# The first groups of the last expert layer are formed one expert earlier, and the later planner's minor steps go last

## Chip, cores and metric

One core of a Trainium2 chip runs the whole program. The metric is the device time of one execution in microseconds (us). Engines: PE multiplies matrices, DVE (VectorE), ACT (ScalarE) and POOL (GpSimd) work on tiles, SP issues most plain DMAs, POOL the indirect ones.

## What is computed

Three layers follow each other. The kernel's names for the inputs are those of the reference.

```python
x = attention(q, k, v)             # 4 x 8 heads, 576 tokens, 64 wide; block-causal; as (2304, 512)
# first expert layer: two of 8 experts for each token, weights from a softmax over those two
noisy = x @ w_gate + log1p(exp(x @ w_noise)) * noise
x2[token] = sum over its two experts e of  gate * (relu(x[token] @ w1[e]) @ w2[e])
# last expert layer: the best of 8 experts for each token
logits = x2 @ w_gate2 + modality_bias[modality_id]
out[token] = softmax(logits)[best] * (relu(x2[token] @ m2w1[best]) @ m2w2[best])
```

With the reference's inputs the first layer gives its experts 620, 582, 567, 546, 540, 559, 608 and 586 rows. In the last layer only two experts are ever best: number 1 for 1165 tokens and number 2 for 1139. A token is complete once both its first-layer experts have run. After experts 0 to 5, 1188 tokens are complete (588 for expert 1 of the last layer, 600 for expert 2); after experts 0 to 6 there are 1718 (866 and 852).

## The kernel before

**Jobs.** After attention, `run` (L1418) goes through a list of jobs: both parts of experts 0 and 1, then experts 2 to 7 of the first layer (`firsts`, L655), then six jobs of the last layer (`seconds`, L657). A job has up to 620 gathered rows, in tiles of 128 or 124. Its first half (`mm1`, L516, PSUM tile `ph`) makes 8 hidden slices with 24 matmuls each, its second half (`mm2`, L535, PSUM tile `py`, three buffers) 24 matmuls for each row tile. All are split into a high and a low part, so every product is three matmuls. Between the row tiles of one job, `between` (L1440) prepares the next: the columns of its rows (`cols`, L503: 4 transposes into `px`, one ACT copy `xth`, one DVE subtraction `xtl`) and its weight splits (`split`, L454: ACT writes `wh`, and `wl` is a subtraction on POOL for the first layer, on DVE or POOL for the last). `rows` (L1425) gathers the next job's rows on POOL's queue (`gather`, L491, tile `xr`), one for each hidden slice, as soon as the flag that it needs is set. SP fetches weights (`fetch`, L443, tile `raw`), four tiles ahead, when the job's expert is known.

**What a first-layer row tile leaves behind.** POOL adds the finished rows `yr` to X2 in DRAM (`add_rows`, L600). DVE then takes eight dot products of the PSUM tile `py` with the last layer's gate weights (`note`, L570; tile `zero<-py,gts,wide`), and POOL adds them, with a count of one, to LG in DRAM. So column `E` of LG says how many of a token's two experts are done. These dots are fed in between other work (`filler`, L558). Before a new row tile, `room` (L553) issues dots until at most 16 are left, and the PSUM buffer of the tile three back has to be read out first.

**The planner of the last layer.** `gates(k)` (L1478) is a chain of some 60 to 100 small DVE steps with a few matmuls in PSUM tile `pt`, fed in step by step (`walk`, L385). It loads LG on SP's queue (`lgx`), picks each token's best expert, masks the tokens that are complete (L1497), counts, forms full groups of 512 rows of one expert, and turns positions into row lists by one-hot matmuls (`sl_ob`, `sl_ov`, `lists`, `slot_ids`). `eg<k>` says which experts' weights to fetch, `ids<k>0` which rows to gather. k=0 forms two groups of 512 from complete tokens. k=1 forms two more of 512 and two small ones of 256, with an overflow plan (`eo`, `gso`, `more`) that only a loop at the end of the program reads. The chain for k=0 is started when the last dots of expert 6 are placed (`then`, L656), that for k=1 after those of expert 7. PE and DVE take their instructions strictly in the order in which this program writes them, so a matmul of the chain that has to wait holds all of PE.

**Order of transfers.** Gathers of the k=0 groups read X2 while expert 7 may still add rows to it. They touch other tokens, so the program tells the scheduler that these transfers don't depend on each other (L495 to L498, L609): `last_rows` holds expert 7's additions, `early_rows` the gathers.

Of the kernel before, what the change touches and what calls it, by code (L numbers as in the profile page):

```python
# [7 lines left out]
F32 = mybir.dt.float32  # L8
F32R = mybir.dt.float32r
BF16 = mybir.dt.bfloat16  # L10
I32 = mybir.dt.int32
AF = mybir.ActivationFunctionType
OP = mybir.AluOpType
AX = mybir.AxisListType.X
# [16 lines left out]
def moe_kernel(tc, q, k, v, w_gate, w_noise, noise, w1, w2, mod_id, w_gate2, mod_bias, m2w1, m2w2, out):  # L31
    nc = tc.nc
    B, H, S, D = q.shape
    NT, DM = out.shape
    E = w_gate.shape[1]
# [3 lines left out]
    NP = CAP // 128  # L39
# [5 lines left out]
    BW, NW, NSM = GW // 128, 2, 2  # L45
    NV = 5
    NA1 = E * NP
    NTT = NT // 128
# [8 lines left out]
    def bc(ap, shape):  # L57
        return ap.to_broadcast(shape)
# [45 lines left out]
    vec, ten, act = Timed(nc.vector, "dve", dve_cost), Timed(nc.tensor, "pe", pe_cost), Timed(nc.scalar, "act", act_cost)  # L104

    with ExitStack() as top:
# [22 lines left out]
        ones = cst.tile([128, 128], BF16, name="ones")  # L129
# [196 lines left out]
        def starts(pool, n, th, pre):  # L326

            nt = th.shape[1]
            ng = pool.tile([128, E, nt], F32, name=pre + "ng")
            vec.tensor_tensor(ng, bc(n[:, :, None], [128, E, nt]), bc(th[:, None, :], [128, E, nt]), op=OP.is_gt)  # L330
            yield .3
            gn = pool.tile([128, E], F32, name=pre + "gn")
            vec.tensor_reduce(gn, ng, axis=AX, op=OP.add)
            yield .3
            st8 = pool.tile([128, E, E], F32, name=pre + "st8")
            vec.tensor_tensor(st8, lt8, bc(gn[:, None, :], [128, E, E]), op=OP.mult)
            yield .3
            gs = pool.tile([128, E], F32, name=pre + "gs")
            vec.tensor_reduce(gs, st8, axis=AX, op=OP.add)
            yield .3  # L340
            return gn, gs

        def experts_of(pool, gn, gs, dst, pre):

            ge = pool.tile([1, NG2, E], F32, name=pre + "ge")
            vec.tensor_tensor(ge, bc(gs[0:1, None, :], [1, NG2, E]), bc(lane[0:1, 0:NG2, None], [1, NG2, E]), op=OP.is_le)
            yield .3
            ef = pool.tile([1, NG2 + 1], F32, name=pre + "ef")
            vec.tensor_reduce(ef[:, 0:NG2], ge[:, :, 1:], axis=AX, op=OP.add)
            yield .3  # L350
            vec.tensor_tensor(ef[:, NG2:], gs[0:1, E - 1:E], gn[0:1, E - 1:E], op=OP.add)
            yield .3
            vec.tensor_copy(dst, ef)
            yield .3
            return ef[:, NG2:]
# [113 lines left out]
        class Job:  # L469
# [21 lines left out]
            def gather(s, t):  # L491
                xr = rp.tile([128, DM], F32, name="xr", bufs=5)
                i = gps.indirect_dma_start(out=xr, out_offset=None, in_=s.table,
                                                 in_offset=bass.IndirectOffsetOnAxis(ap=s.ic(t), axis=0))
                if s.apart is not None:  # L495
                    for o in s.apart:
                        tc.declare_no_dep(i.ins, o.ins, reason="rows of other tokens")
                    early_rows.append(i)  # L498
                s.xr.append(xr)
                if s is j11:  # L500
                    s.due.append(max(clk["dve"], clk["pool"]) + 2.5)
# [96 lines left out]
        last_rows, early_rows = [], []  # L598

        def add_rows(ids, c0, nt, then=None):  # L600
            last = c0 + nt == NA1
            prev = last_rows if last else []
            placed_ = []

            def f(t, yr, py, g):
                c = c0 + t
                i = gps.indirect_dma_start(out=X2, out_offset=bass.IndirectOffsetOnAxis(ap=ids[:, c:c + 1], axis=0),
                                                 in_=yr, in_offset=None, compute_op=OP.add)
                for o in prev + (early_rows if last else []):  # L609
                    tc.declare_no_dep(i.ins, o.ins, reason="rows of other tokens")  # L610
                prev.append(i)
                note(yr, py, g, ids[:, c:c + 1], placed_, then if t == nt - 1 else None)
            return f

        def job1(e, t0=0, nt=NP, then=None, need=(None, None)):
            return Job((w1[e], w2[e]), X1, nt, lambda t: ids1[:, e * NP + t0 + t:e * NP + t0 + t + 1],
                       lambda t: gts1[:, e * NP + t0 + t:e * NP + t0 + t + 1], add_rows(ids1, e * NP + t0, nt, then), need, 128 if nt == 2 else UNIT)
# [35 lines left out]
        j11.wa, j11.wb = j10.wa, j10.wb  # L653
        chain = lambda k, p: lambda: walk(gates(k), now[0] + .5, p)
        firsts = [job1(0, FIRST[0], NP - FIRST[0], need=(None, "ids1"))]  # L655
        firsts += [job1(e, then={E - 2: chain(0, 1), E - 1: chain(1, 1)}.get(e), need=(None, "ids1")) for e in range(2, E)]  # L656
        seconds = [job2(k, g) for k in range(2) for g in range(NW)] + [job2(1, g, True) for g in range(NSM)]  # L657
        stage = Stage([j00, j10] + firsts + seconds)

# [818 lines left out]
        def gates(k):  # L1478
# [37 lines left out]
            if k == 1:  # L1516
                nr = pool.tile([128, E], F32, name="g_nr")
                vec.scalar_tensor_tensor(nr, gn, -float(GW), pp[:, NTT], op0=OP.mult, op1=OP.add)
                yield .3
                gm, gr = yield from starts(pool, nr, th2, "q_")  # L1520
                yield from experts_of(pool, gm, gr, egs, "q_")
                flags.add("egs")
                vec.tensor_scalar(gr, gr, 2.0, float(BW * NW), op0=OP.mult, op1=OP.add)
                yield .3
                vec.scalar_tensor_tensor(gr, gn, -float(BW), gr, op0=OP.mult, op1=OP.add)
                yield .3
                vec.tensor_add(nr, gs, gn)
                yield .3
                vec.tensor_scalar(nr, nr, NW + .5, 1e5, op0=OP.is_gt, op1=OP.mult)
                yield .3  # L1530
                vec.tensor_add(gs, gs, nr)
                yield .3
                go, s_ = yield from starts(pool, base, th1, "o_")
                vec.tensor_copy(gso, s_)
                yield .3
                yield from experts_of(pool, go, gso, eo, "o_")
            t0, pos, st = tl("t0", sh), tl("pos"), tl("st")
            vec.tensor_tensor(t0, pp[:, 0:NTT], oh, op=OP.mult)
            yield .3
# [14 lines left out]
                vec.scalar_tensor_tensor(w, s2, float(GW), pos, op0=OP.mult, op1=OP.is_gt)  # L1554
                yield .3
            if k == 1:
                vec.tensor_tensor(t0, oh, bc(gr[:, None, :], sh), op=OP.mult)
                yield .3
                vec.tensor_reduce(s2, t0, axis=AX, op=OP.add)
                yield .3  # L1560
                vec.scalar_tensor_tensor(st, st, float(BW), s2, op0=OP.mult, op1=OP.subtract)
                yield .3
                vec.tensor_tensor(st, st, w, op=OP.mult)
                yield .3
                vec.tensor_add(st, st, s2)
                yield .3
# [7 lines left out]
            if k < 2:  # L1574
                new = tl("new") if k else placed
                vec.tensor_scalar(new, a, cap - .5, None, op0=OP.is_lt)
                yield .3
                if k:
                    vec.tensor_add(placed, placed, new)
                    yield .3  # L1580
                    held = tl("held", dt=BF16)
                    vec.tensor_copy(held, placed)
                    yield "pe", 0
                    pm = ps_r.tile([128, NTT], F32, name="pt")
                    ten.matmul(pm, ones, held, start=True, stop=True)
                    yield .4
                    m = pool.tile([1, 1], F32, name="g_m")
                    vec.tensor_reduce(m, pm[0:1], axis=AX, op=OP.add)
                    yield .3
                    vec.tensor_scalar(more, m, float(NT) - .5, None, op0=OP.is_lt)  # L1590
                    yield .3

            vec.tensor_tensor(l, l, bc(mx[:, :, None], sh), op=OP.subtract)
# [11 lines left out]
            for i0_, a0 in enumerate(range(0, cap, 2 * HG)):  # L1605
                na = min(2 * HG, cap - a0)
                pl = ps_r.tile([128, NV, na], F32, name="pt")
                for i in range(2):
                    n = slice(HN * i, HN * i + HN)
                    ob = yield from hot_b(pool, bl[:, n], HN)  # L1610
                    ov = yield from hot_a(pool, a[:, n], HN, a0, na, vals2[:, n])
                    yield from lists(pl, ob, ov, HN, i == 0, i == 1)
                acc = pool.tile([128, NV, na], F32, name="g_acc")
                vec.tensor_copy(acc, pl)
                yield .3
                yield from slot_ids(pool, acc, na, NTT, pad2[:, a0:a0 + na], ids[:, a0:a0 + na], gts[:, a0:a0 + na])
                flags.add("ids%d%d" % (k, i0_ > 0))
            flags.discard("chain")

        with sp():  # L1620
# [131 lines left out]
```

## Time and profile before

| | |
|---|---|
| three runs | 983.49 us median (981.95 to 984.66) |
| the profiled execution | 984.59 us, span 982.8 us |
| PE busy | 943.6 us (96%) |
| DVE, ACT, POOL busy | 681.4 (69%), 482.6 (49%), 489.6 us (50%) |
| share of PE in the chain that ended last | 70% |
| DMA | mean 127 GB/s over the span |

A number such as "668.18" in what follows is a time in us from the start of the span. The rows of a window view give, for each stretch, the busy time of each engine and in brackets its instructions. PEclk is the granted share of PE's full clock (1.00 is 2.4 GHz, 0.50 is 1.2 GHz). A timeline row gives start, duration, engine, line, operation and tiles (out<-in), then in square brackets how long the engine was idle just before, and who ended that. L73 is a helper's line through which every operation goes, so tiles tell them apart.

The stretches of interest: expert 6 takes PE from 610.54 to 668.18, expert 7 to 737.85, the four groups of 512 rows to 785.16, 841.80, 887.25 and 931.74, then come the two small groups.

### The profile page before, as it was taken

How to read it: one execution, taken by the hardware profiler on the slowest of the kernel's cores; microseconds unless marked ns; L12 is line 12 of the kernel's file. 1: busy time of each engine (PE TensorE's matmuls, PEld its weight loads, DVE VectorE, ACT ScalarE, POOL GpSimd, SP SyncE). 2: the span in 40 equal slices, each digit the busy share in tenths (PEclk: the TensorE clock that was granted, in tenths of full speed). 3: DMA queues.
4: the chain of work that ended last, by engine and by line, in shares of the span. 5: the costliest groups of instructions: out<-in, count | busy, mean ns of one | idle time of the engine just before them, and what ended most of it. 6: DMA issues, size and time to landing. Idle time of an engine off the chain costs nothing.

```text
span 982.8 us, 16351 instructions
## 1 busy us (share of the span) xinstructions
PE 943.6 (96%) x5661; PEld 835.6 (85%) x5661; DVE 681.4 (69%) x1676; ACT 482.6 (49%) x1090; POOL 489.6 (50%) x472
## 2 busy tenths in 40 slices
PE   9999998999999999999999999999889988999995
PEld 6989897998978999989898998989767876888894
DVE  6878779888889979395775939577877764433241
ACT  6989997987651344333333333433223332433352
POOL 6234343464325599585875848557374124222122
PEclk9999999999999999999999999999999999999998
DMA  6586742322196366374654627443554525443440
GB/s 128 104 216 192 233 122 70 78 60 68 58 337 156 68 187 165 111 158 97 130 128 116 122 76 171 99 76 47 161 113 124 181 79 175 137 130 108 138 130 13
DMA packets 145293, 124.49 MB, mean 127 GB/s; under 512 B 75626, under 2 KB 115946, under 8 KB 145075
## 3 DMA queue, kind: packets, MB, share of 16 engines
q1 hardware_dynamic: 126242, 90.14, 32.0%
q0 software_dynamic: 17904, 32.96, 16.7%
q8 instruction: 47, 0.77, 0.3%
q10 hardware_dynamic: 1056, 0.26, 0.1%
q14 instruction: 44, 0.35, 0.1%
HBM read 95.50 MB, written 28.09 MB: 126 GB/s over the span
## 4 chain that ended last, share of the span: by engine, by line
PE 70%; issue 11%; DVE 6%; POOL 5%; ACT 4%; DMA 3%; SPq 0%; POOLq 0%; ACTq 0%; DVEq 0%
PE py L73 25%; PE ph L73 25%; PE pt L73 8%; PE ps L73 6%; PE pa L73 3%; POOL wl L73 2%; PE px L73 2%; ACT p L73 2%; DMA raw<-in_moe_w_dram 1%; DVE wl L73 1%; DMA xr<-X,ids 1%; DVE PTl L73 1%; ACT kp L73 1%; DMA qld<-in_q_dram 1%; POOL out_dram L73 1%
## 5 line engine op out<-in xcount | busy, mean ns | idle before, releaser
L73 POOL TENSOR_TENSOR wl<-raw,wh 128x1024 fp32r<-128x1024 f32 x70 | 180.9, 2602 | 113.8 <-ACT wh L73 111.2
L73 DVE SCALAR_TENSOR_TENSOR zero<-py,gts,wide 128x512 f32<-128x512 f32 x304 | 227.6, 749 | 8.4
L73 PE MATMUL ph<-xth,wh 128*128 128x312 f32 (+4 forms) x672 | 217.2, 323 | 2.1 <-DVE kp L73 1.2
L73 PE MATMUL ph<-xtl,wh 128*128 128x312 f32 (+4 forms) x672 | 216.9, 323 | 0.2 <-DVE xtl L73 0.2
L73 PE MATMUL ph<-xth,wl 128*128 128x312 f32 (+4 forms) x672 | 217.1, 323 | 0.0
L73 PE MATMUL py<-wh,kp 128*128 128x512 f32 x488 | 166.0, 400 | 0.0
L73 PEld LDWEIGHTS ph<-xth,wh 128*128 128x128 f32 x672 | 127.4, 190 | 8.5 <-DVE kp L73 1.9
L73 PEld LDWEIGHTS ph<-xtl,wh 128*128 128x128 f32 x672 | 127.3, 189 | 6.0 <-DVE xtl L73 0.5
L73 PEld LDWEIGHTS ph<-xth,wl 128*128 128x128 f32 x672 | 126.9, 189 | 5.2
L73 ACT ACTIVATE yr<-py,gts 128x512 f32<-128x512 f32 x59 | 40.6, 688 | 165.0 <-PE py L73 109.3
L73 ACT ACTIVATE wh<-raw 128x1024 fp32r<-128x1024 f32 x112 | 117.8, 1052 | 2.1 <-DMA raw<-in_moe_w_dram 2.1
L73 PEld LDWEIGHTS py<-wh,kp 128*128 128x128 f32 x488 | 92.4, 189 | 19.0
L73 DVE SCALAR_TENSOR_TENSOR hl<-ph,hh 128x312 fp32r<-128x312 f32 (+5 forms) x84 | 43.0, 514 | 78.8 <-ACT hh L73 78.7
L73 PE MATMUL ps<-kh,kp 128*128 128x256 f32 (+5 forms) x320 | 95.9, 340 | 0.5 <-ACT p L73 0.3
L73 PE MATMUL py<-wl,kp 128*128 128x512 f32 x244 | 96.0, 394 | 0.0
L73 PE MATMUL py<-wh,hh 128*128 128x512 f32 x228 | 94.3, 413 | 0.0
L73 POOL DMA_INDIRECT xr<-X,ids x54 | 56.1, 1040 | 76.2 <-PE px L73 43.3
L73 PE MATMUL py<-wh,hl 128*128 128x512 f32 x228 | 90.9, 399 | 0.0
L73 PE MATMUL py<-wl,hh 128*128 128x512 f32 x228 | 90.5, 397 | 0.0
L73 ACT ACTIVATE hh<-ph 128x312 fp32r<-128x312 f32 (+5 forms) x84 | 38.4, 457 | 99.8 <-PE ph L73 99.6
L73 DVE TENSOR_TENSOR xtl<-px,xth 128x512 fp32r<-128x512 f32 (+1 forms) x57 | 38.9, 682 | 64.6 <-ACT xth L73 64.6
L73 ACT ACTIVATE kp<-ph 128x312 fp32r<-128x312 f32 (+5 forms) x84 | 38.4, 457 | 91.8 <-PE ph L73 91.4
(274 smaller groups left out, 1843.0 us busy)
## 6 DMA issues: line engine op xcount, KB each, us to landing
raw<-in_moe_w_dram SPq DMA_DIRECT2D x112, 512.0 KB, 3.6
X<-zero SPq DMA_DIRECT2D x13, 512.0 KB, 4.0
kld<-in_k_dram SPq DMA_DIRECT2D x32, 128.0 KB, 2.9
vld<-in_v_dram SPq DMA_DIRECT2D x32, 128.0 KB, 2.8
X<-x SPq DMA_DIRECT2D x16, 256.0 KB, 2.7
qld<-in_q_dram SPq DMA_DIRECT2D x30, 128.0 KB, 3.0
wide<-in_moe_w_dram SPq DMA_DIRECT2D x4, 512.0 KB, 5.7
wide<-WG2T POOLq DMA_DIRECT2D x1, 2048.0 KB, 10.2
```

The costliest lines, as they stand in the source:

```text
L73: return f(*a, **kw)
```

## The change

The chain for k=0 is started by expert 5's last dots instead of expert 6's. `last_rows` becomes a list of two lists, the additions of expert 6 and those of expert 7, and both are declared independent of the early gathers. In the chain for k=1 four things move to the end: the experts of the small groups go behind the list of the first 8 row tiles, and the overflow plan (16 small DVE steps in all, with one small matmul, `g_held`) behind all lists. The numbers that were kept in `gr` go to a tile of their own, `gb`, since `gr` is now read later.

```diff
@@ -493,7 +493,7 @@
                 i = gps.indirect_dma_start(out=xr, out_offset=None, in_=s.table,
                                                  in_offset=bass.IndirectOffsetOnAxis(ap=s.ic(t), axis=0))
                 if s.apart is not None:
-                    for o in s.apart:
+                    for o in sum(s.apart, []):
                         tc.declare_no_dep(i.ins, o.ins, reason="rows of other tokens")
                     early_rows.append(i)
                 s.xr.append(xr)
@@ -598,15 +598,16 @@
         last_rows, early_rows = [], []
 
         def add_rows(ids, c0, nt, then=None):
-            last = c0 + nt == NA1
-            prev = last_rows if last else []
-            placed_ = []
+            late = c0 >= (E - 2) * NP
+            prev, placed_ = [], []
+            if late:
+                last_rows.append(prev)
 
             def f(t, yr, py, g):
                 c = c0 + t
                 i = gps.indirect_dma_start(out=X2, out_offset=bass.IndirectOffsetOnAxis(ap=ids[:, c:c + 1], axis=0),
                                                  in_=yr, in_offset=None, compute_op=OP.add)
-                for o in prev + (early_rows if last else []):
+                for o in prev + (early_rows if late else []):
                     tc.declare_no_dep(i.ins, o.ins, reason="rows of other tokens")
                 prev.append(i)
                 note(yr, py, g, ids[:, c:c + 1], placed_, then if t == nt - 1 else None)
@@ -653,7 +654,7 @@
         j11.wa, j11.wb = j10.wa, j10.wb
         chain = lambda k, p: lambda: walk(gates(k), now[0] + .5, p)
         firsts = [job1(0, FIRST[0], NP - FIRST[0], need=(None, "ids1"))]
-        firsts += [job1(e, then={E - 2: chain(0, 1), E - 1: chain(1, 1)}.get(e), need=(None, "ids1")) for e in range(2, E)]
+        firsts += [job1(e, then={E - 3: chain(0, 1), E - 1: chain(1, 1)}.get(e), need=(None, "ids1")) for e in range(2, E)]
         seconds = [job2(k, g) for k in range(2) for g in range(NW)] + [job2(1, g, True) for g in range(NSM)]
         stage = Stage([j00, j10] + firsts + seconds)
 
@@ -1518,11 +1519,10 @@
                 vec.scalar_tensor_tensor(nr, gn, -float(GW), pp[:, NTT], op0=OP.mult, op1=OP.add)
                 yield .3
                 gm, gr = yield from starts(pool, nr, th2, "q_")
-                yield from experts_of(pool, gm, gr, egs, "q_")
-                flags.add("egs")
-                vec.tensor_scalar(gr, gr, 2.0, float(BW * NW), op0=OP.mult, op1=OP.add)
-                yield .3
-                vec.scalar_tensor_tensor(gr, gn, -float(BW), gr, op0=OP.mult, op1=OP.add)
+                gb = pool.tile([128, E], F32, name="g_gb")
+                vec.tensor_scalar(gb, gr, 2.0, float(BW * NW), op0=OP.mult, op1=OP.add)
+                yield .3
+                vec.scalar_tensor_tensor(gb, gn, -float(BW), gb, op0=OP.mult, op1=OP.add)
                 yield .3
                 vec.tensor_add(nr, gs, gn)
                 yield .3
@@ -1530,10 +1530,6 @@
                 yield .3
                 vec.tensor_add(gs, gs, nr)
                 yield .3
-                go, s_ = yield from starts(pool, base, th1, "o_")
-                vec.tensor_copy(gso, s_)
-                yield .3
-                yield from experts_of(pool, go, gso, eo, "o_")
             t0, pos, st = tl("t0", sh), tl("pos"), tl("st")
             vec.tensor_tensor(t0, pp[:, 0:NTT], oh, op=OP.mult)
             yield .3
@@ -1554,7 +1550,7 @@
                 vec.scalar_tensor_tensor(w, s2, float(GW), pos, op0=OP.mult, op1=OP.is_gt)
                 yield .3
             if k == 1:
-                vec.tensor_tensor(t0, oh, bc(gr[:, None, :], sh), op=OP.mult)
+                vec.tensor_tensor(t0, oh, bc(gb[:, None, :], sh), op=OP.mult)
                 yield .3
                 vec.tensor_reduce(s2, t0, axis=AX, op=OP.add)
                 yield .3
@@ -1577,17 +1573,6 @@
                 yield .3
                 if k:
                     vec.tensor_add(placed, placed, new)
-                    yield .3
-                    held = tl("held", dt=BF16)
-                    vec.tensor_copy(held, placed)
-                    yield "pe", 0
-                    pm = ps_r.tile([128, NTT], F32, name="pt")
-                    ten.matmul(pm, ones, held, start=True, stop=True)
-                    yield .4
-                    m = pool.tile([1, 1], F32, name="g_m")
-                    vec.tensor_reduce(m, pm[0:1], axis=AX, op=OP.add)
-                    yield .3
-                    vec.tensor_scalar(more, m, float(NT) - .5, None, op0=OP.is_lt)
                     yield .3
 
             vec.tensor_tensor(l, l, bc(mx[:, :, None], sh), op=OP.subtract)
@@ -1615,6 +1600,25 @@
                 yield .3
                 yield from slot_ids(pool, acc, na, NTT, pad2[:, a0:a0 + na], ids[:, a0:a0 + na], gts[:, a0:a0 + na])
                 flags.add("ids%d%d" % (k, i0_ > 0))
+                if k == 1 and i0_ == 0:
+                    yield from experts_of(pool, gm, gr, egs, "q_")
+                    flags.add("egs")
+            if k == 1:
+                go, s_ = yield from starts(pool, base, th1, "o_")
+                vec.tensor_copy(gso, s_)
+                yield .3
+                yield from experts_of(pool, go, gso, eo, "o_")
+                held = tl("held", dt=BF16)
+                vec.tensor_copy(held, placed)
+                yield "pe", 0
+                pm = ps_r.tile([128, NTT], F32, name="pt")
+                ten.matmul(pm, ones, held, start=True, stop=True)
+                yield .4
+                m = pool.tile([1, 1], F32, name="g_m")
+                vec.tensor_reduce(m, pm[0:1], axis=AX, op=OP.add)
+                yield .3
+                vec.tensor_scalar(more, m, float(NT) - .5, None, op0=OP.is_lt)
+                yield .3
             flags.discard("chain")
 
         with sp():
```

## Rows read from the trace of the kernel before

**Rows 1.** Windows view by stage: expert 6, expert 7, groups 0, 1 and 2.

```profile
core 0: us, PE busy (x) PEld busy (x) DVE busy (x) ACT busy (x) POOL busy (x), PEclk, DMA share, GB/s
...
610.54:668.18 57.64, 57.64 (x333) 52.18 (x332) 39.66 (x102) 20.64 (x34) 35.51 (x19) 1.00 0.48 99
668.18:737.85 69.67, 62.97 (x366) 54.54 (x364) 54.78 (x147) 21.34 (x35) 41.69 (x26) 0.95 0.45 105
737.85:785.16 47.31, 46.87 (x228) 38.46 (x228) 36.67 (x96) 16.61 (x23) 15.77 (x11) 1.00 0.52 149
785.16:841.80 56.64, 51.33 (x247) 40.01 (x245) 31.55 (x73) 17.61 (x25) 19.32 (x15) 0.94 0.42 130
841.80:887.25 45.45, 45.45 (x209) 37.62 (x208) 15.89 (x19) 17.30 (x24) 10.67 (x8) 1.00 0.44 138
```

**Rows 2.** Waits of PE from 640 us on: total us, times, longest us.

```profile
PE px L73 <- DMA xr<-X,ids: 4.5, 3, 2.8
PE pt L73 <- DVE sl_ov L73: 2.7, 1, 2.7
PE pt L73 <- DVE g_held L73: 2.5, 1, 2.5
PE px L73 <- DVE xtl L73: 1.4, 1, 1.4
PE ph L73 <- ACT xth L73: 0.9, 1, 0.9
```

**Rows 3.** Windows view of a stretch behind a wait in expert 7.

```profile
708.55:711.97 3.42, 3.42 (x16) 2.52 (x17) 3.28 (x9) 0.00 (x0) 0.00 (x0) 0.50 0.51 153
```

**Rows 4.** Timeline of PE: expert 6's fifth row tile, and two waits in group 1.

```profile
662.61 0.40 PE L73 MATMUL py<-wh,kp 128*128 128x512 f32 x1
...
795.99 0.18 PE L73 MATMUL pt<-g_held,ones 128*128 128x18 bf16 x1 [2.51 <-DVE g_held L73]
...
820.95 0.93 PE L73 MATMUL px<-ident,xr 128*128 128x128 f32 x4 [2.80 <-DMA xr<-X,ids]
```

**Rows 5.** Timeline of POOL and SP: last dots of experts 5, 6, 7; the chains' loads.

```profile
623.63 1.56 POOL L73 DMA_INDIRECT LG<-yg,ids  x1 [1.43 <-DVE zero L73]
...
681.32 1.56 POOL L73 DMA_INDIRECT LG<-yg,ids  x1 [1.48 <-DVE zero L73]
...
684.44 0.34 SPq L1489 DMA_DIRECT2D lgx<-LG  x1
...
764.32 1.56 POOL L73 DMA_INDIRECT LG<-yg,ids  x1 [5.21 <-DVE zero L73]
...
767.23 0.34 SPq L1489 DMA_DIRECT2D lgx<-LG  x1
```

**Rows 6.** Timeline of POOL and DVE: a weight split beside steps of the chains.

```profile
700.53 2.40 POOL L73 TENSOR_TENSOR wl<-raw,wh 128x1024 fp32r<-128x1024 f32 x1 [7.55 <-ACT wh L73]
...
700.63 2.38 DVE L73 TENSOR_TENSOR vals<-g_t,vals 128x18 bf16<-128x18 f32 x1
...
704.41 4.02 DVE L73 TENSOR_TENSOR sl_ov<-sl_oa,vals 128x360 bf16<-128x360 bf16 x1
...
714.28 0.53 DVE L73 TENSOR_TENSOR sl_ov<-sl_oa,vals 128x360 bf16<-128x360 bf16 x1
...
792.50 2.32 DVE L73 TENSOR_TENSOR sl_a<-sl_a,g_msk 128x18 f32<-128x18 f32 x1
```

**Rows 7.** DVE: expert 6's column steps (lines view), last dots of second row tiles (timeline).

```profile
L73 DVE TENSOR_TENSOR xtl<-px,xth 128x496 fp32r<-128x496 f32 x4 | 2.7, 673 | 5.6 <-ACT xth L73 5.6
...
659.49 0.75 DVE L73 SCALAR_TENSOR_TENSOR zero<-py,gts,wide 128x512 f32<-128x512 f32 x1
...
722.68 0.75 DVE L73 SCALAR_TENSOR_TENSOR zero<-py,gts,wide 128x512 f32<-128x512 f32 x1
```

**Rows 8.** Timeline of DVE: the first row lists of both chains.

```profile
719.95 0.16 DVE L73 TENSOR_TENSOR ids<-si_t,si_u 128x8 int32<-128x8 f32 x1
...
815.99 0.17 DVE L73 TENSOR_TENSOR ids<-si_t,si_u 128x8 int32<-128x8 f32 x1
```

## The prediction

> **What bounds the kernel now.** I read the windows view by stage first [rows 1]. Two stages with the same work should take the same time. Experts 6 and 7 have nearly the same (PE's 333 instructions against 366, the rest being small matmuls of the planner's chain), yet the one takes 57.64 us and the other 69.67. In expert 6 PE is busy from end to end at full clock; in expert 7 it is idle for 69.67 - 62.97 = 6.7 us and has a mean clock of 0.95. Groups 1 and 2 of the last layer differ alike: 56.64 us with 51.33 busy at 0.94, against 45.45 without a gap. So PE bounds this part of the kernel, and there is nothing to win except these gaps and what they do to the clock. DVE, at 39.66 of 57.64 us in expert 6, has room, though not much.
>
> The view of PE's waits says who ends the gaps [rows 2]. In expert 7 a one-hot step of the chain (`sl_ov`) holds the chain's matmuls for 2.7 us. At the end of expert 7 the rows of group 0 come late: `xr` 4.5 - 2.8 = 1.7 us (the longest of its three waits, 2.8, is in group 1 [rows 4]), then `xtl` 1.4 and `xth` 0.9 behind it. Together that is 6.7, the idle time found above. In group 1 `g_held` costs 2.5 and the late rows of group 2 cost 2.8 [rows 4], together 5.3, again the whole idle time.
>
> Behind the longer gaps the clock falls: 3.42 us at 0.50, which is 1.2 GHz [rows 3], so 1.7 us of work is lost each time. The mean of 0.95 over 69.67 us is 3.5 us, two such falls; 0.94 over 56.64 is 3.4, two more.
>
> **Why the rows are late.** The chain for group 0 starts when the last dots of expert 6 are in LG (681.32, load at 684.44) [rows 5] and has its row list at 719.95 [rows 8], when expert 7, which ends at 737.85, is in its last third and gathers and column steps are still to come. The chain for groups 2 and 3 starts at 767.23 [rows 5] and has its first list at 815.99 [rows 8], when the gap before group 2's columns (820.95 - 2.80 = 818.15) is almost there [rows 4].
>
> **The change, part by part.**
>
> *Earlier start for k=0.* Expert 5's last dots are placed at 623.63, 57.69 us before expert 6's [rows 5], and expert 6's stage is 57.64 us long. The chain therefore starts 16 us into expert 6, just as it now starts 16 us into expert 7, and should have its list near 719.95 - 57.7 = 662.3, before expert 7 begins at 668.18. The four gathers of group 0 then go out in expert 7's first half. They pass on POOL's queue ahead of that half's weight splits, which are needed only in the second half: that hides them, and without this cover each would cost up to the 1.56 us of POOL's other indirect DMAs [rows 5]. Weight fetches of group 0 on SP, now held back until the chain has named the expert, come earlier too. The early LG load sits on SP's queue, where fetches stand behind it; up to four fetched weight tiles cover that, so I cost it at nothing. The groups stay what they were: after expert 5 the two experts have 588 and 600 complete tokens, enough for 512 each, and what is left (653 and 627) again gives one full group and one small one each.
>
> Expert 7 then looks like expert 6: 69.67 - 57.64 = **12.0 us less**. Of this 6.7 is idle time, 3.5 the clock, and 1.8 the chain's own small matmuls, which move to expert 6: **1.8 more** there.
>
> *What the chain does to expert 6.* Since it starts at the same point of the stage, its tail meets the second half of expert 6, in which DVE must read out a PSUM buffer for every row tile; the fifth tile waits for the second's dots. In expert 6 these dots end at 660.24 and the fifth tile starts at 662.61 [rows 4, 7]: 2.4 us to spare. In expert 7, with the chain, they end at 723.43 [rows 7], that is 665.7 when moved back by 57.7. Two corrections: the one-hot step took 4.02 us instead of the 0.53 of its twin [rows 6], which held the dots up by 3.5 and need not happen again; and expert 6 has five column steps of 0.67 us in this half [rows 7], which in expert 7 came later: 3.4 more. That gives 665.6. PE, with about 1 us of chain matmuls by then, wants its buffer at 663.6. So I expect a new wait of 2.0 us, and one fall of the clock of 1.7: **3.7 more**. Its ends: nothing, if the 2.38 us step `vals` [rows 6] also falls back to the 0.16 or 0.17 us of other small steps [rows 8]; 5.5 + 1.7 = 7.2, if the 3.5 are lost again. I take the middle case, since one such collision of the two in expert 7 is nearest to what the rows show elsewhere (one in the k=1 chain).
>
> Here is a row that speaks against the change. `vals` started at 700.63 and ended with the weight split that POOL ran from 700.53 to 702.93 [rows 6]; `sl_a`, too, took 2.32 us. Expert 6's second half has four such splits. The Trainium skill (SBUF — State Buffer, "Who interferes with whom") says that a VectorE instruction with two SBUF inputs contends with a GpSimd instruction that reads SBUF, and that the later of the two blocks fully. By that rule the chain is held wherever it meets a split, and the sum goes to the upper end; the trace agrees for `vals`.
>
> *k=1: the later start that becomes an earlier one.* Expert 7's dots no longer queue behind a chain, so they should end as expert 6's do, 681.32 - 668.18 = 13.1 us into the next stage, against 764.32 - 737.85 = 26.5 now [rows 1, 5]: 13.4 us sooner. The 16 DVE steps that go last are written 0.3 us apart (4.8), and `g_held` no longer holds anything ahead of the list (2.5). Group 2's list, now 815.99 - 785.16 = 30.8 us into group 1, should come about 10 us into it, well before its rows are wanted. Both gaps of group 1 go: 5.3 us and the clock's 3.4, **8.7 less**; the other 2.5 us by which it exceeds group 2 are the chain's matmuls and stay somewhere.
>
> `g_held` still stands on PE's queue, later, and the chain meets other splits. One collision like the present one costs 2.5 + 1.7 = 4.2; none costs nothing, two 8.4. I take half of one, **2.1 more**, as the present chain had one such collision.
>
> *Sum:* 12.0 - 1.8 - 3.7 + 8.7 - 2.1 = 13.1 less. The profiled execution took 984.59 us, so 971.5; it stands 1.1 above the median of the three runs, so on their scale **970.4**.
>
> **The rivals.**
>
> *A: POOL holds the chain in both places.* Expert 6 loses 7.2 and k=1 the full 4.2: 12.0 - 1.8 - 7.2 + 8.7 - 4.2 = 7.5 less, 976.0. For it: both chains now are hit. Against: POOL has only 15.77 us of work in group 0 [rows 1], where the k=1 chain will largely run. The Trainium skill's rule above would have it come out so in expert 6. Chance 0.20.
>
> *B: all is hidden.* No new wait: 12.0 - 1.8 + 8.7 = 18.9 less, 964.6. Against it: both corrections above would have to be wrong in the same direction. Chance 0.10.
>
> *C: the change doesn't do what it says.* Some remaining order between the early gathers and the additions of expert 6 or 7 keeps group 0's rows late; then the 4.0 us of gaps and one fall of 1.7 at the end of expert 7 stay: 7.4 less, 976.1. Chance 0.05.
>
> *D: slower, by the chain's matmuls on PE's queue.* The chains have nine places where PE stops for DVE: two counts, two list halves for k=0, four for k=1, and `g_held`. Two of the nine are late now [rows 2]. DVE's work in expert 6 becomes 54.78 of 57.64 us if the chain's share of expert 7 moves there [rows 1], so it could be late at most of them, at 4.2 each. Four or five late places eat the 18.9 (no change), six make it 6.3 slower, 989.8; that is where it decides. Against it: the same chain met the same load in expert 7 and was late once. Chance 0.07 (0.04 slower, 0.03 the same).
>
> **How the numbers follow.** My forecast has the remaining 0.58, with its own range from 966.5 to 974. The range of 965 to 977.5 takes in A, C and half of B, and leaves out the rest of B, D and the tail of A, about 0.2. What a measurement of this kernel can tell from no change is about 0.3%, or 3 us. Forecast, A, B and C all lie beyond that, at 0.93 together, less 0.03 for tails: faster 0.90; the same 0.03 + 0.03 = 0.06; slower 0.04.
>
> **What would show it.** In the changed profile: the first `lgx` load near 627; group 0's gathers in expert 7's first half and no idle time before its columns; expert 7 within a us of expert 6's present 57.64; expert 6 longer by some 5 us, its one longer wait being `py` for DVE's dots or a list matmul; dots of expert 7 done about 13 us into group 0; group 2's list some 10 us into group 1, without a gap before its columns; PEclk at half speed twice or less between 610 and 930 instead of four times. The prediction is wrong if gaps move rather than go: if expert 6 takes 65 us or more, if `g_held` or a list waits for 2 us or more at several places, or if expert 7 still ends in a wait for `xr`.

## The result, and the profile after

The changed kernel takes 967.72 us in the median (966.35 to 968.28), against 982.72 (980.44 to 984.66) for the kernel before, measured beside it: a ratio of 0.9837, 95% interval 0.9812 to 0.9861. That is 15.0 us less, or 16.0 by the ratio on the 983.49 us from which the prediction was made, which would be 967.5. 970.4 was predicted, with a range of 965.0 to 977.5. The profiled execution took 966.35 us, its span is 964.6. Executions of the kernel before differ more among themselves: the thirteen beside the first two sets of experiments took 980.05 to 984.50 us, the five shortest (up to 980.92) at a mean granted clock of 0.992 or 0.993 and the others (from 982.10) at 0.989 to 0.991; the one that was profiled, 984.59 us at 0.989, is a long one.

The windows view of the changed kernel, cut at its own stages (expert 6, expert 7, groups 0, 1 and 2; columns as in [rows 1]):

```profile
609.66:671.51 61.85, 59.99 (x370) 53.22 (x369) 53.38 (x149) 20.96 (x35) 37.32 (x22) 1.00 0.46 107
671.51:728.73 57.22, 57.22 (x330) 51.80 (x329) 41.15 (x105) 20.10 (x33) 42.97 (x24) 1.00 0.56 120
728.73:775.40 46.67, 46.46 (x228) 38.36 (x227) 35.71 (x99) 17.63 (x25) 14.23 (x10) 1.00 0.48 139
775.40:823.60 48.20, 47.63 (x247) 38.08 (x246) 30.46 (x65) 17.29 (x24) 19.94 (x15) 1.00 0.53 165
823.60:869.05 45.45, 45.45 (x210) 37.63 (x208) 15.66 (x18) 17.30 (x24) 10.66 (x8) 1.00 0.42 129
```

Expert 7 now takes 57.22 us instead of 69.67, PE busy throughout; group 1 takes 48.20 instead of 56.64. Expert 6 pays 4.2 us (61.85 against 57.64). DVE's busy time shows the chain's move directly: 53.38 us in expert 6 and 41.15 in expert 7, where [rows 1] have 39.66 and 54.78. PE's clock is 1.00 in all five stretches. The sum of the five is 17.3 us less than in [rows 1]. The two profiled spans differ by 0.9 more, which arises before expert 6 begins (609.66 against 610.54) and is no work of the change. The stages set one profile against one, and the profile before is of a long execution; by the runs the change is worth 15.0 to 16.0 us.

PE's waits from 600 us on, of which [rows 2] showed 12.0 us, are these (columns as there):

```profile
PE pt L73 <- DVE sl_ov L73: 1.1, 2, 0.7
PE py L73 <- DVE zero L73: 0.9, 1, 0.9
PE px L73 <- DVE xtl L73: 0.4, 1, 0.4
PE pt L73 <- DVE g_oh L73: 0.2, 1, 0.2
```

Late rows and `g_held` are gone from the list. A wait that was not there before is `py` for `zero`: a row tile waits for the PSUM buffer that the dots of the tile three back still read.

The steps of the two chains in the timelines of SP, DVE and POOL (compare [rows 5, 8]):

```profile
625.81 0.34 SPq L1490 DMA_DIRECT2D lgx<-LG  x1
...
660.73 0.17 DVE L73 TENSOR_TENSOR ids<-si_t,si_u 128x8 int32<-128x8 f32 x1
...
662.35 1.02 POOL L73 DMA_INDIRECT xr<-X,ids  x1 [0.30 <-issue]
...
749.45 1.56 POOL L73 DMA_INDIRECT LG<-yg,ids  x1 [0.15 <-DVE hl L73]
...
752.36 0.34 SPq L1490 DMA_DIRECT2D lgx<-LG  x1
...
792.25 0.17 DVE L73 TENSOR_TENSOR ids<-si_t,si_u 128x8 int32<-128x8 f32 x1
```

The k=0 chain loads LG at 625.81 and has its list at 660.73, 11 us before expert 7 begins. The k=1 chain loads at 752.36 and has its first list at 792.25, 16.9 us into group 1.

### The profile page after: what moved, and what is told of

It reads as the page before. It is cut to its first block, busy times and chain, and to the rows that moved or that the text cites. A ratio compares the mean times of both kernels' runs of the same rounds, so it can differ in the third digit from the quotient of the medians.

```text
span 964.6 us, 16355 instructions
## 1 busy us (share of the span) xinstructions
PE 936.1 (97%) x5661; PEld 832.2 (86%) x5661; DVE 679.2 (70%) x1676; ACT 482.6 (50%) x1090; POOL 491.4 (51%) x472
## 5 line engine op out<-in xcount | busy, mean ns | idle before, releaser
L73 ACT ACTIVATE p<-ps,nm 128x288 f32<-128x288 f32 (+8 forms) x160 | 79.2, 500 | 7.2 <-DVE nm L73 6.2
```

The source lines that it names most:

```text
L73: return f(*a, **kw)
```

## The experiments

All ran beside the kernel before. Ratios are to it; where a few us matter, the text says with which runs of the changed kernel a time is compared (967.72 us, ratio 0.9837, at first; 968.78 us, ratio 0.9830, later on the second chip, where 966 to 968 and near 0.984 were expected). Three experiments are single runs without an interval; they rest on what their traces show.

### The early start alone

The `then` of expert 5 (shown) and the second list of additions (as in the change, not shown again), with the k=1 chain's steps left in their old order:

```diff
-        firsts += [job1(e, then={E - 2: chain(0, 1), E - 1: chain(1, 1)}.get(e), need=(None, "ids1")) for e in range(2, E)]
+        firsts += [job1(e, then={E - 3: chain(0, 1), E - 1: chain(1, 1)}.get(e), need=(None, "ids1")) for e in range(2, E)]
```

> The early start alone: the k=0 chain begins behind expert 5, the 16 minor steps and g_held stay ahead of the first list of the k=1 chain. Theory (the early start does most, and by itself brings the k=1 chain forward, since expert 7's dots no longer queue behind a chain): experts 6 and 7 as in the changed kernel (61.9 and 57.2 us), k=1 load near 752 as there, first list 5 to 8 us later than its 792, so group 2's rows land at 802 to 804, where PE wants them at 802: a wait of 0 to 2.5 us, and g_held late or not. In all 0 to 5 us slower than the changed kernel, 967.5 to 973. Rival (the moved minor steps win group 1's time): group 1 keeps both its gaps and its clock falls, 8.7 us more than the changed kernel, 976.

969.26 us, ratio 0.9875 (0.9856 to 0.9894). Experts 6 and 7 and group 0 are those of the changed kernel to 0.02 us. Only group 1 differs. Its window:

```profile
775.22:826.40 51.18, 49.20 (x246) 38.95 (x245) 28.85 (x63) 17.38 (x25) 19.63 (x15) 0.97 0.47 147
```

The timeline of the same run has the DVE step that was held up, PE's longest wait behind it, and the first list:

```profile
783.52 2.15 DVE L73 CAST vals<-g_t 128x18 bf16<-128x18 f32 x1
...
788.40 0.24 PE L73 MATMUL pt<-sl_ov,sl_ob 128*128 128x40 bf16 x3 [1.98 <-DVE sl_ov L73]
...
801.00 0.17 DVE L73 TENSOR_TENSOR ids<-si_t,si_u 128x8 int32<-128x8 f32 x1
```

By the medians this is 1.5 us slower than the changed kernel (967.72), and the intervals of the two ratios overlap; in the profiles group 1 is 3.0 us longer: a wait of 1.98 (0.47 there) and 0.03 of 51.18 us of clock, 1.5 us. The list is there at 801.00, 25.8 us into the group instead of 16.9. That much later it was expected; the rows were still in time, without a wait for `xr`. What PE waits for is a one-hot step behind a small step (`vals`, 2.15 us) that was held up. So the theory's size is right and the place is another: the moved minor steps are worth 1.5 us by the medians and 3.0 us in the profiles beside the early start, here by which of the chain's steps are held, not by the rows.

### The minor steps last alone

The changed kernel with the old `then`; the additions of expert 6 are no longer declared independent either (`late` from `E - 1` on, not shown):

```diff
-        firsts += [job1(e, then={E - 3: chain(0, 1), E - 1: chain(1, 1)}.get(e), need=(None, "ids1")) for e in range(2, E)]
+        firsts += [job1(e, then={E - 2: chain(0, 1), E - 1: chain(1, 1)}.get(e), need=(None, "ids1")) for e in range(2, E)]
```

> The minor steps last alone: the k=0 chain begins behind expert 6 as before. Theory: expert 7 keeps its 12 us (waits at the list and for the rows, two clock falls); the k=1 chain still begins near 767, but its first list comes some 7 us sooner (809 instead of 816), in time for the rows at 818, and g_held holds nothing there: group 1 loses its 8.7 us. 974, halfway. Rival (the minor steps are off PE's path and only the chain's start decides): no change from before, 982.

975.47 us, ratio 0.9941 (0.9918 to 0.9964), as the theory had it. The windows of expert 7 and group 1:

```profile
667.88:736.59 68.71, 61.51 (x366) 53.58 (x365) 54.70 (x147) 21.31 (x35) 41.84 (x26) 0.98 0.45 106
783.89:833.40 49.51, 47.94 (x246) 37.65 (x245) 32.16 (x75) 17.49 (x25) 19.45 (x15) 1.00 0.51 161
```

And of two stretches behind waits, one in expert 7 and one at its end:

```profile
708.14:712.00 3.86, 3.86 (x24) 3.05 (x25) 3.72 (x11) 0.69 (x1) 0.13 (x1) 1.00 0.51 136
730.47:733.88 3.41, 3.41 (x11) 2.83 (x10) 1.98 (x4) 0.60 (x1) 2.85 (x3) 0.50 0.61 111
```

Expert 7 keeps its waits (7.2 us idle). Group 1 falls from 56.64 to 49.51 us. So each part alone repairs most of group 1 (5.5 us for the early start, 7.1 for the minor steps, 8.4 for both); the early start repairs expert 7 as well. In group 1 the gains don't add up. In the whole time this can't be told: 1.25% and 0.59% come to 1.84% where both together give 1.63%, with intervals of about 0.2% on each.

The last two windows hold a surprise. At 708.14 PE had just waited 2.65 us for the same list as in the kernel before at 708.49 (2.70 us), and the clock stayed at 1.00; there it fell to 0.50 [rows 3]. Whether the kernels differ in this, or only the two executions, isn't shown: with one profile of each, and mean clocks from 0.989 to 0.993 among executions of the kernel before, it may be either.

### Declared independence, for one expert less, and for none

```diff
-            late = c0 >= (E - 2) * NP
+            late = c0 >= (E - 1) * NP
```
```diff
-            if k == 0:
-                j.apart = last_rows
```

> The changed kernel, with only expert 7's additions to X2 declared independent of the early gathers, so that group 0's gathers wait for expert 6's last addition to land. Theory (the gathers have some 35 us to spare: issued at 662 to 670, wanted near 706): they go out near 678 instead, nothing on PE moves, same as the changed kernel within 1 us, 967 to 969. Rival (the declared independence of expert 6 is what makes the early rows early): group 0's rows are late again, or POOL's weight splits behind the waiting gathers are, 4 to 6 us slower, 972 to 974.

> The changed kernel with no additions declared independent of the early gathers. Group 0's gathers are then issued behind expert 6's last addition and ahead of expert 7's; group 1's wait for expert 7's last addition to land, near 735, and are wanted near 751. Theory (after the early start nothing is left for the declared independence to save): within 1 us of the changed kernel. Rival (early rows need it): group 1's rows late, or POOL's later work held behind the waiting gathers; 3 to 10 us slower.

966.15 us, ratio 0.9844 (0.9825 to 0.9863), and 968.17 us, 0.9828 (0.9810 to 0.9847): both the same as the changed kernel, which on the second chip took 968.78, ratio 0.9830 (0.9815 to 0.9846). The early gathers move as expected. The timeline of POOL has the first one of group 0 with expert 7 alone independent:

```profile
678.18 1.02 POOL L73 DMA_INDIRECT xr<-X,ids  x1 [2.04 <-issue]
```

With none independent, the first one of group 1:

```profile
737.83 1.01 POOL L73 DMA_INDIRECT xr<-X,ids  x1 [3.52 <-DMA X<-yr,ids]
```

In the changed kernel these two are the gathers at 662.35 (above) and the fifth one:

```profile
669.75 0.94 POOL L73 DMA_INDIRECT xr<-X,ids  x1 [0.30 <-issue]
```

The first goes out 16 us later than there and the second 68 us later, and in both runs PE has the same waits as in the changed kernel, none of them for rows. After the early start, declaring the additions independent saves nothing: by order alone the rows are in time. What it saved before the change no run shows.

### The chain spread out, and packed

Pace 2 writes the k=0 chain's steps half as dense, pace 0.5 twice as dense, 0.75 was combined with the freer dots of the next section:

```diff
-        firsts += [job1(e, then={E - 3: chain(0, 1), E - 1: chain(1, 1)}.get(e), need=(None, "ids1")) for e in range(2, E)]
+        firsts += [job1(e, then={E - 3: chain(0, 2), E - 1: chain(1, 1)}.get(e), need=(None, "ids1")) for e in range(2, E)]
```

> The changed kernel, with the k=0 chain's steps written half as dense (pace 2 instead of 1), so that its tail goes into expert 7, where DVE has idle time and the list is still 15 us ahead of its need. Theory (expert 6's new waits, 0.65 at the list and 0.85 for the PSUM buffer, come from the chain's tail crowding the dots): these waits go, 1 to 2 us faster than the changed kernel, 966 to 967. Rival (the tail crowds expert 7's dots in the same way, and expert 7's last dots and the k=1 chain get later): the waits move to expert 7, and group 2's rows become late, 0 to 3 us slower.

972.82 us, ratio 0.9910 (0.9889 to 0.9930): 5.1 us slower than the changed kernel by the medians, 7.2 by the ratios. Both theories were wrong: the waits neither went nor moved to expert 7, they grew in expert 6. Its window, and PE's two waits in the timeline:

```profile
609.34:677.07 67.73, 62.10 (x352) 54.96 (x351) 51.00 (x128) 20.98 (x35) 35.55 (x19) 0.95 0.41 94
...
659.68 0.50 PE L73 MATMUL py<-wh,kp 128*128 128x512 f32 x1 [2.84 <-DVE zero L73]
...
669.85 0.50 PE L73 MATMUL py<-wh,kp 128*128 128x512 f32 x1 [2.78 <-DVE zero L73]
```

DVE's steps of the chain that took over 2 us, in the same run:

```profile
642.92 2.35 DVE L73 TENSOR_TENSOR g_st<-lt,g_gn 128x64 f32<-128x64 f32 x1
...
649.24 2.43 DVE L73 TENSOR_SCALAR sl_a<-sl_a 128x18 f32<-128x18 f32 x1
...
659.83 2.06 DVE L73 CAST vals<-g_mx 128x18 bf16<-128x18 f32 x1
...
669.71 2.47 DVE L73 TENSOR_TENSOR sl_oa<-lane,sl_a 128x72 bf16<-128x72 f32 x1
```

Four small steps of 0.2 us take over 2 us, one for each of POOL's four weight splits in this half. A longer chain meets more of them. That they make the two waits is argued from the order: two held steps come before the first wait and one between the two, while the fourth begins only 0.14 us before the second wait ends.

> The changed kernel with the k=0 chain's steps written twice as dense (pace 0.5), so that more of it is done before expert 6's second half, where POOL's weight splits and the dots are. Theory (what pace 2 cost came from four steps of the chain meeting a POOL split, about 2.2 us each; at pace 1 there are two): at most one step is held, the two waits of 0.65 and 0.85 us shrink or go, 0.5 to 2 us faster than the changed kernel, ratio 0.982 to 0.983. Rival (pace 2 cost because the chain as a whole, which lets fewer dots through while it lasts, lasted longer, or because dense steps outrun DVE and PE meets them early): the same as the changed kernel or up to 2 us slower, a count matmul or list waiting longer.

967.85 us, ratio 0.9850 (0.9826 to 0.9874): not to be told from the changed kernel. In its trace expert 6 takes 63.63 us instead of 61.85. One step was held (2.23 us), and the waits for the columns and the buffer went, as the theory said, but others came early, as the rival said. PE's waits from 600 to 700 us:

```profile
PE ph L73 <- DVE hl L73: 2.0, 2, 1.1
PE pt L73 <- DVE g_oh L73: 1.0, 1, 1.0
PE pt L73 <- DVE sl_ov L73: 0.6, 1, 0.6
```

> An attempt at a better kernel: the changed kernel with the k=0 chain's pace at 0.75, between 1 (a wait of 0.85 for a PSUM buffer late in expert 6) and 0.5 (three waits early in it), and with dots let through freely. Theory (all of expert 6's waits are worth 1.85 us, and each pace trades early against late ones): 0 to 1 us faster than the changed kernel measured beside it, not resolved by the rounds. Rival (there is a place between where neither appears): 1.5 to 2 us faster.

> The changed kernel once more, beside the others: 966 to 968, ratio to before near 0.984.

The pace of 0.75 takes 973.77 us, ratio 0.9882 (0.9865 to 0.9898), against 968.78 and 0.9830 for the changed kernel on the same chip: 5 us slower, with one wait of 4.1 us for the list, and 6.8 us at half clock behind it. Both theories were wrong: this pace is no better place between (the freer dots alone, in the next section, cost nothing). Which steps meet a split changes with the pace: here they are three others (`g_ge`, `sl_oa` and `si_u`, 1.92 to 2.28 us).

### Dots let through sooner

```diff
-            while fill and "places" in flags and (len(fill) > 30 or fill[0][0] <= clk["pe"] and clk["dve"] < clk["pe"] + (.2 if "chain" in flags else .4)):
+            while fill and "places" in flags and (len(fill) > 30 or fill[0][0] <= clk["pe"] and clk["dve"] < clk["pe"] + .4):
```

> The changed kernel, with dots let through while a chain runs as freely as without one (DVE's lead over PE of 0.4 instead of 0.2 us in the planner's own clock). Theory (order of the dots is a small matter; DVE is full in expert 6's second half whichever goes first): within 1 us of the changed kernel, ratio 0.983 to 0.985, the waits moving between list and buffer. Rival (the dots are late because the chain holds them back by that rule): the buffer wait of 0.85 goes, and expert 7's last dots, 21 us into group 0, come earlier; 1 to 2 us faster.

966.08 us, ratio 0.9831 (0.9807 to 0.9856): the same. The buffer wait shrinks from 0.85 to 0.62, and expert 7's last dots are placed 20.7 us into group 0, exactly as late as in the changed kernel.

### A suspected place delayed

```diff
                     ob = yield from hot_b(pool, bl[:, n], HN)
+                    for _ in range(2 if k == 0 and i == 0 else 0):
+                        nc.vector.tensor_tensor(ob, bc(lane[:, None, :], [128, HN, 128]), bc(bl[:, n][:, :, None], [128, HN, 128]), op=OP.is_equal)
```

> The changed kernel with two more one-hot steps (1.35 us each) on DVE ahead of the k=0 chain's first list, written twice into the same tile and unknown to the order's planner. Theory (that place has no slack: PE waits there 0.65 us already, and the dots behind it feed the buffer wait of 0.85): PE's wait at the list grows by about 2.7 us to 3.3, the clock falls once, the buffer wait stays near 0.85: 3 to 5 us slower than the changed kernel, 970 to 972. Rival (DVE has room at that place): 0 to 1 us slower.

970.03 us in one run, 2.3 us more than the changed kernel's median; expert 6 takes 64.57 us instead of 61.85. PE's only wait from 600 to 700 us:

```profile
PE pt L73 <- DVE sl_ov L73: 3.4, 1, 3.4
```

Expert 6's window in that run:

```profile
610.65:675.22 64.57, 61.13 (x370) 54.29 (x369) 56.08 (x151) 20.96 (x35) 35.67 (x21) 0.97 0.43 99
```

The 2.7 us added to DVE come out as 2.8 us of wait: the place has no slack. The clock fell once, and in the time that PE lost, DVE caught up with its dots, so that the two later waits (0.35 and 0.85) vanished; the expectation had the second of them stay.

### Is it POOL's splits, or DVE's load?

First the four splits of expert 6's second half were put on DVE, in the kernel of pace 2:

```diff
-                            stage.split(ea[left[1] % len(ea)] if "ids1" in flags else vec)
+                            stage.split(ea[left[1] % len(ea)] if "ids1" in flags and j is not firsts[-2] else vec)
```

> The kernel of pace 2, with the four weight splits of expert 6's second half on DVE (1.22 us each) instead of POOL (2.4). Theory (POOL's splits hold the chain's steps, which costs pace 2 its two buffer waits of 2.8 us and two falls of the clock): the four steps that took 2.1 to 2.5 us take their usual 0.2 to 0.3, which frees 8.5 us of DVE against 4.9 added; the two waits shrink to 1 us or less each and the clock does not fall, 3 to 6 us faster than pace 2. Rival (it is DVE's load that makes the waits): with 4.9 us more work on DVE the waits stay or grow, 0 to 5 us slower than pace 2.

981.33 us in one run, 8.5 us more than pace 2, and no small step was held. By the expectation's letter the rival wins, though 8.5 us lies beyond its 0 to 5. But the trace names another reason. PE's wait for a buffer from 600 to 700 us:

```profile
PE py L73 <- DVE zero L73: 13.0, 2, 8.5
```

DVE's wait for ACT from 640 to 690 us:

```profile
DVE wl L73 <- ACT wh L73: 7.9, 4, 6.2
```

A split on DVE waits for ACT's `wh`, which stands on ACT's queue behind `yr`, which waits for PE, which waits for the dots behind the split. DVE was idle, not full. So this run shows that without splits on POOL in this half no step of the chain is held there, but not what the held steps cost PE, and the question was asked the other way: POOL does each of the four splits twice, and nothing changes for the other engines.

```diff
+                        if j is firsts[-1] and w == "a":
+                            nc.gpsimd.tensor_sub(lo[:, d], raw[:, c:c + k], hi[:, d].bitcast(F32))
```

> The changed kernel, with POOL doing each of the four weight splits of expert 6's second half twice, into the same tile; what PE, ACT and DVE do and their order stay. Theory (a POOL split holds a chain step of DVE that reads two tiles of SBUF until the split ends): instead of two steps held for 3.5 us together, two to four are held, up to 4.8 us each, and PE's waits in expert 6, 1.85 us now, grow to 4 to 9 us, with one or two falls of the clock; 3 to 10 us slower than the changed kernel. Rival (DVE's own load and the order of its dots make the waits): DVE's steps keep their times and PE's waits stay within 1 us of 1.85.

972.37 us in one run, 3.6 us more than the changed kernel on this chip (968.78), and expert 6 takes 66.20 us instead of 61.85. PE's waits from 600 to 700 us:

```profile
PE pt L73 <- DVE sl_ov L73: 2.8, 1, 2.8
PE px L73 <- DVE xtl L73: 1.0, 1, 1.0
PE py L73 <- DVE zero L73: 0.9, 1, 0.9
```

Expert 6's window:

```profile
611.42:677.62 66.20, 61.52 (x370) 54.30 (x369) 57.73 (x149) 20.94 (x35) 42.91 (x23) 0.97 0.38 86
```

Two steps of DVE which in the changed kernel take 0.22 us each, beside the two added splits of POOL that fall into the chain (L468; the other two come behind the list):

```profile
647.45 3.43 POOL L468 TENSOR_TENSOR wl<-raw,wh 128x1024 fp32r<-128x1024 f32 x1
...
648.60 2.38 DVE L73 TENSOR_TENSOR sl_oa<-lane,sl_a 128x72 bf16<-128x72 f32 x1
...
656.89 3.40 POOL L468 TENSOR_TENSOR wl<-raw,wh 128x1024 fp32r<-128x1024 f32 x1
...
657.95 2.44 DVE L73 TENSOR_TENSOR sl_oa<-lane,sl_a 128x72 bf16<-128x72 f32 x1
```

Four steps are held instead of two, DVE's busy time grows by 57.73 - 53.38 = 4.35 us without a single instruction more, and PE's waits grow from 1.85 to 4.7 us, with one fall of the clock. Each of the two steps ends within 0.1 us of the split beside it. So POOL's splits hold DVE's small steps, and through them PE. How much of the changed kernel's own 1.85 us they make is not shown: no run took the splits away without other harm.

## Why the prediction was right

*Expert 7, 12.0 us less:* 12.45. The mechanism and the size hold; the small matmuls moved with the chain, as PE's count shows (366 to 330, and 333 to 370 in expert 6). They cost more than the 1.8 us of the sum: PE's busy time in expert 6 grew by 59.99 - 57.64 = 2.35 us. As they also leave expert 7, the two errors all but cancel.

*Earlier start:* the load was expected near 627 and the list near 662.3; they came at 625.81 and 660.73. The gathers did not wait for expert 7's first half, as was said, but went out from 662.35 on: the program fixes the order of the other engines, while POOL's is left to the scheduler.

*Expert 6, 1.8 for the matmuls and 3.7 for a new wait:* 4.2 in all, 2.35 and 1.85. The wait of 2.0 us is there, cut into three (0.65 at the list, 0.35 at the columns, 0.85 for the buffer), and the clock did not fall behind them. The 1.7 us for the clock is the term that was too large. The second tile's dots ended at 665.81, where 665.6 was forecast; that it comes so close is in part luck, as a step was held that the forecast did not have: the correction that decided between 3.7 and 7.2 held (`sl_ov` was not held again, `vals` was), but a second one-hot step, `sl_ob`, took twice its time. Both stand beside a split of POOL, here in the timelines of DVE and POOL of the changed kernel:

```profile
643.21 2.40 POOL L73 TENSOR_TENSOR wl<-raw,wh 128x1024 fp32r<-128x1024 f32 x1 [8.75 <-ACT wh L73]
...
643.25 2.43 DVE L73 TENSOR_TENSOR vals<-g_t,vals 128x18 bf16<-128x18 f32 x1
...
647.56 0.52 DVE L73 TENSOR_TENSOR sl_ov<-sl_oa,vals 128x360 bf16<-128x360 bf16 x1
...
650.52 2.40 POOL L73 TENSOR_TENSOR wl<-raw,wh 128x1024 fp32r<-128x1024 f32 x1 [2.17 <-ACT wh L73]
...
651.51 2.62 DVE L73 TENSOR_TENSOR sl_ob<-lane,sl_b 128x1152 bf16<-128x1152 f32 x1
```

*k=1, first list about 10 us into group 1:* 16.9. The step that failed is that expert 7's last dots would end 13.1 us into the next stage, as expert 6's do: it was 20.7. Group 0's first half isn't an expert's: DVE has weight splits there too, and is busy for 17.33 us of the 21.93 that the window of the changed kernel takes in:

```profile
728.73:750.66 21.93, 21.93 (x98) 18.19 (x97) 17.33 (x39) 8.68 (x12) 10.76 (x7) 1.00 0.46 113
```

Freer dots changed nothing, and why it is 20.7 and not somewhat less stays open. The other two terms of this sum, 4.8 and 2.5 us, held: with the minor steps last alone the list came 23.3 us into group 1 instead of 30.8. The late dots cost nothing, as 16.9 us is early enough, and the early start alone bore a list at 25.8.

*Group 1, 8.7 less, and 2.1 for a new collision of k=1:* 8.4 less in all. One wait of 0.47 us is left, and no fall of the clock. The 2.1 was half of the one collision that the chain had before; three runs show that it is the luck of the order (0.47, 1.98 with the minor steps first, 1.27 with them last and the late start).

By the stages the gain is 17.3 us where the sum had 13.1: 1.3 more in expert 6 (4.2 paid instead of 5.5, the clock above all), 1.8 in group 1 (8.4 instead of 8.7 - 2.1), 0.6 in group 0, which the sum had left alone, and 0.5 in expert 7. By the runs it is 15.0 to 16.0. The sum took its four falls of the clock, some 7 us, from one long execution of the kernel before, and corrected only the level for that (the 1.1 us); by their clocks of up to 0.993 other executions had less to win, though which falls they were spared no profile shows. So the forecast comes as near as it does in part by luck: it priced its collisions too high, and what there was to win from the clock too high as well. Rival A, POOL holding the chain, is a true mechanism, shown by the doubled splits; at pace 1 it costs expert 6 at most the 1.85 us of all its waits, and not the 5.5 of wait and 1.7 of clock that the rival had. Rival C fell in the strongest form: with no independence declared the rows are in time. Rival D stayed away: of nine places PE stops noticeably (0.3 us or more) at two.

## What to carry to other kernels

When an engine waits for a planning chain that runs beside it, starting the chain one stage earlier on less complete data can remove the wait, as it did here, provided the data then suffice to fill the work. Ask first where the chain's small steps will stand: here each small step of DVE could be held by a long operation of POOL, and what was queued behind it paid. Two remedies for one wait need not add up (5.5 and 7.1 us in group 1 came to 8.4), so cost each with the other in place; and try whether a safeguard (here the declared independence) still pays once the wait is gone.

## What was not expected of the hardware

The clock's falls can't be told from a wait's length alone. It fell to half behind waits of 2.70, 2.51 and 2.80 us in the kernel before, 1.98 (early start alone), 2.84 and 2.78 (pace 2), and stayed up behind 2.65 at the same list (minor steps last alone). Behind single waits of 1.3 us or less it stayed up in these traces, yet it also fell at the end of expert 7 in the kernel before, behind a group of waits of 1.45, 0.27 and 1.41 us. Two of these, and the stretch behind them:

```profile
725.83 0.66 PE L73 MATMUL px<-ident,xr 128*128 128x128 f32 x4 [1.45 <-DMA xr<-X,ids]
...
731.55 0.66 PE L73 MATMUL px<-ident,xr 128*128 128x128 f32 x4 [1.41 <-DVE xtl L73]
...
732.45:735.86 3.41, 3.41 (x9) 2.66 (x9) 2.88 (x7) 0.39 (x1) 3.08 (x3) 0.50 0.76 133
```

So a sum that adds 1.7 us for each wait of 2 to 3 us should carry that as a bound, not as a price; behind the wait of 4.1 us (pace 0.75) the clock stayed at half for 6.8 us, twice as long.

Not only steps with two inputs are held by POOL: at pace 2 a `TENSOR_SCALAR` (2.43 us) and a `CAST` (2.06 us) with one input of 128x18 were, beside a split each. The Trainium skill (SBUF — State Buffer, "Who interferes with whom") names these among the operations that can take the shared ports; the trace agrees. The dots, with one input in PSUM, kept their 0.75 us beside every split.
